# Splitting q and k for fp32r score products: the duplicated load, VectorE and GpSimd, or one load, ScalarE, VectorE and DMAs between partitions

## The chip, the core and the metric

The kernel runs on one core of a Trainium2 chip. The metric is the device time of one execution in microseconds; lower is better. A run's time is the median of several executions.

## What is computed

Attention over 8 batches of 8 heads, 576 positions and 64 channels a head, with a learned bias on relative positions, then a mixture of 8 experts of which each token uses one:

```python
scores = q @ k.T / sqrt(64) + bias        # bias: a small MLP of log1p|i-j| / log1p(max(i,1))
attn = softmax(scores)
x = (attn @ v) laid out as 4608 tokens x 512
e = argmax(x @ w_gate)
out = softmax_prob(e) * (relu(x @ w1[e]) @ w2[e])
```

Everything is float32. The score products run in the faster fp32r form, which keeps fewer bits; so q and k are split into a rounded part and a remainder, and the products of the parts are added up.

## The kernel before

**The stages.** The first 109 us make the bias for all heads (`bias_group`, 36 groups of 16 rows) and, between them, the first pairs of heads. Then 28 pairs pass one after another in a pipeline (`attend_units`), the last two pairs interleaved, up to about 745 us; then come the experts (`Experts`).

**One pair.** A pair is two heads of one batch, five tiles of q rows (four of 128, one of 64). For each tile and head: four score products of 128 x 288 into PSUM (`product`, line 163); VectorE adds the bias and takes the row minimum (line 168); ScalarE takes the exponential and the row sum (line 171); TensorE transposes the result (208, 203), ScalarE and VectorE copy it to SBUF (214, 204, 212, 210); TensorE multiplies it with v (219, 222). The steps of neighbouring tiles overlap: the transposes of one tile stand behind the score products of the next. The `s` tiles in PSUM and the `tps` tiles have two buffers each.

**q and k.** In HBM both lie transposed, with the two heads side by side (1216 columns), and the 64 channels twice, in partitions 0 to 63 and 64 to 127. `load_qk` (lines 125 to 143) loads each with one DMA of 608 KB. VectorE casts k to fp32r (line 138); GpSimd subtracts that from k in the upper 64 partitions (139), so that `k1` holds the rounded part above the remainder. VectorE casts q (141), GpSimd subtracts it in all partitions (142): `q1` is the rounded part twice, `q2` the remainder twice. A product with `q1` and one with `q2`, each over 128 partitions, add up to all four products of parts. `q1`, `q2`, `k1` and `v` have two buffers (pool `kq`), the raw tiles two (pool `raw`).

**What sets the order.** `ahead` asks for `load_qk` of the next pair at the second q tile of a pair, and for `load_v` at the fourth. The framework's scheduler then orders the instructions of each engine, and inserts the waits; each engine works through its list in order. All these loads stand on SP's queue. The framework has eight completion semaphores for the DMAs, so a DMA can wait for the one eight before it on that queue.

Of the kernel before, what the change touches and what calls it, by code (L numbers as in the profile page):

```python
# [10 lines left out]
F32 = mybir.dt.float32  # L11
F32R = mybir.dt.float32r
I32 = mybir.dt.int32
AF = mybir.ActivationFunctionType
ALU = mybir.AluOpType
# [5 lines left out]
P = 128  # L21
B, H, S, D = 8, 8, 576, 64
SH = S // 2
NPAIR = H // 2
# [4 lines left out]
QT = len(QN)  # L29
KC = DM // P  # L30
FC = FF // P
KW = 2 * S + 64
NG = S // 16
XW = DM + 4

# [42 lines left out]
def attention(tc, ctx, q, kt, vm, ltab, bcst, gate, gt, cm, cmat, ival, tail0, pcst, bias, xs, plan, moe):  # L78
    nc = tc.nc
    ident, before, ones = gt[:, 0, :P], cm[:, 0], cm[:, 1]  # L80
    kq = ctx.enter_context(tc.tile_pool(name="kq", bufs=2))
    raw = ctx.enter_context(tc.tile_pool(name="raw", bufs=2))
    tp = ctx.enter_context(tc.tile_pool(name="tp", bufs=2))
    ap = ctx.enter_context(tc.tile_pool(name="ap", bufs=2))
    const = ctx.enter_context(tc.tile_pool(name="aconst", bufs=1))
# [28 lines left out]
    loaded = {}  # L114

    def load_pair(b, pr):
        load_qk(b, pr)
        load_v(b, pr)
# [6 lines left out]
    def load_qk(b, pr):  # L125
        u = b * NPAIR + pr

        def twice(src):

            t = raw.tile([P, KW], F32, name="qk")  # L130
            nc.sync.dma_start(out=t, in_=src[b, pr])
            return t

        q1 = kq.tile([P, KW], F32R, name="q1")
        q2 = kq.tile([P, KW], F32R, name="q2")
        k1 = kq.tile([P, KW], F32R, name="k1")
        t = twice(kt)
        nc.vector.tensor_copy(out=k1, in_=t)  # L138
        nc.gpsimd.tensor_tensor(out=k1[64:128], in0=t[64:128], in1=k1[64:128].bitcast(F32), op=ALU.subtract)  # L139
        t = twice(q)  # L140
        nc.vector.tensor_copy(out=q1, in_=t)  # L141
        nc.gpsimd.tensor_tensor(out=q2, in0=t, in1=q1.bitcast(F32), op=ALU.subtract)  # L142
        loaded[u] = (q1, q2, k1)

    xsb = {}

    def scores(b, pr, qt):

        q1, q2, k1, v = loaded[b * NPAIR + pr]
        n = QN[qt]  # L150
        q0 = qt * P
        if (b, qt) not in xsb:
            xsb[b, qt] = xp[b % 2].tile([P, XW], F32, name="xrow")
        a = ap.tile([P, 2 * S], F32, name="a")
# [3 lines left out]
        def product(hf, hh, second, first, last):  # L158
            if n < P:
                i, k0 = (S - n, S)[hh], (0, KW - S)[hh]  # L160
            else:
                i, k0 = (0, KW - 512)[hh] + q0, S * hh
            return nc.tensor.matmul(s[:, hf, :SH], (q1, q2)[second][:, i:i + P], k1[:, k0 + hf * SH:k0 + hf * SH + SH], start=first, stop=last)  # L163

        def weights(m, hh, bt):

# [6 lines left out]
        if n < P:  # L173
            s = ps_s.tile([P, 2, 512], F32, name="s")
# [8 lines left out]
        for hh in range(2):  # L183
            s = ps_s.tile([P, 2, 512], F32, name="s")
# [301 lines left out]
    with ExitStack() as es:  # L486
        atp = [es.enter_context(tc.tile_pool(name="atp", bufs=2)), es.enter_context(tc.tile_pool(name="osb", bufs=2)), P]
        bp = es.enter_context(tc.tile_pool(name="bp", bufs=1))
        hp = es.enter_context(tc.tile_pool(name="hp", bufs=8))
        op = es.enter_context(tc.tile_pool(name="op", bufs=3))  # L490
        lt = bp.tile([P, 1152], F32, name="lt")
        bc = bp.tile([P, 4 * NG + 2 + 4 * H], F32, name="bc")
# [101 lines left out]
    last = attend_units(units, ahead, after)  # L594
    advance(100)
    plan_experts()
    s = []
# [238 lines left out]
def layout(inputs):  # L836

    q, k, v = inputs["q"], inputs["k"], inputs["v"]

    q, k = (a.reshape(B, NPAIR, 2, S, D).transpose(0, 1, 4, 2, 3).reshape(B, NPAIR, D, 2 * S) for a in (q, k))  # L840

    q = q.reshape(B, NPAIR, D, 2, S).copy()
    q[..., S - 64:] = q[..., S - 64:].reshape(B, NPAIR, D, 2, 8, 8).swapaxes(-1, -2).reshape(B, NPAIR, D, 2, 64)
    q = np.concatenate([q[..., 0, :], np.zeros_like(q[..., 0, :64]), q[..., 1, 512:], q[..., 1, :512]], axis=-1)
    k = np.concatenate([k, k[..., S:S + KW - 2 * S]], axis=-1)

    q, k = (np.concatenate([a, a], axis=2) for a in (q, k))
    vv = v.reshape(B, NPAIR, 2, S, D)
    vm = np.zeros((B, NPAIR, P, 5, P), v.dtype)
    for hh in range(2):  # L850
        h = slice(64 * hh, 64 * hh + 64)
# [8 lines left out]
    t = np.arange(1152)  # L860
    ltab = np.log1p(np.abs(t[None, :] - (S - 1) - 8 * ii[:, None]).astype(np.float32)).astype(np.float32)
    i = np.array([row_base(G, j) for G in range(NG) for j in range(4)])[None, :] + 8 * ii[:, None]
# [42 lines left out]
```

## Time and profile before

| | us |
|---|---|
| median of 3 runs | 1237.55 (1236.25 to 1239.64) |
| the profiled execution | 1246.06 |
| its span, first to last instruction | 1244.2 |
| TensorE matmuls busy | 1111.9 (89%) |
| TensorE weight loads busy | 893.6 (72%) |
| VectorE busy | 776.5 (62%) |
| ScalarE busy | 524.4 (42%) |
| GpSimd busy | 347.3 (28%) |
| 124.57 MB moved by DMA | 100 GB/s over the span |

The shares are means over stages that differ; VectorE for instance is at 80 to 90% up to about 745 us and at about 30% behind it. A busy TensorE isn't TensorE at its peak, because matmuls overlap in it. Names: PE is TensorE's matmuls, PEld its weight loads, DVE is VectorE, ACT is ScalarE, POOL is GpSimd, SP is SyncE, whose queue starts the DMAs.

### The profile page before, as it was taken

The page shows a single profiled execution, that of the slowest core. Times are in us where ns is not written, and L with a number is a line of the kernel's source. Part 1 is how long each engine was busy: PE and PEld are TensorE (multiplying, and loading weights), DVE is VectorE, ACT ScalarE, POOL GpSimd, SP SyncE. Part 2 cuts the span into 40 slices and gives each one's busy share as a digit, 9 for nine tenths or more (in the row PEclk, how much of TensorE's full clock was granted, in tenths as well). Part 3 has the DMA queues.
Part 4 walks back from the last instruction along what each step waited for, and adds up shares of the span by engine and source line. Part 5 has one row for each costly group of instructions (what it writes and reads, how often), then busy time and mean ns, then how long its engine had stood idle before and what let it go on. Part 6 is the DMA issues. An engine that isn't in the chain of part 4 may idle for free. (4 is left out here: it accounts for less than half of the span.)

```text
span 1244.2 us, 20226 instructions
## 1 busy us (share of the span) xinstructions
PE 1111.9 (89%) x7332; PEld 893.6 (72%) x7332; DVE 776.5 (62%) x2025; ACT 524.4 (42%) x1251; POOL 347.3 (28%) x288
## 2 busy tenths in 40 slices
PE   7898888989898888889898899799989899989894
PEld 3457666767666666667676688688978799978782
DVE  8987888898888888887878786232323322324141
ACT  5885655646455555555464463111211211213130
POOL 3003325143333242242333332330005040032320
PEclk8998999999999999999999999899999999999897
DMA  8544213223232232141232241720151610252400
GB/s 237 149 121 122 88 65 110 82 73 119 72 107 78 79 101 92 62 130 62 91 101 87 67 160 65 280 81 26 34 186 44 210 67 23 71 189 68 162 18 26
DMA packets 39362, 124.57 MB, mean 100 GB/s; under 512 B 5154, under 2 KB 5666, under 8 KB 39074
## 3 DMA queue, kind: packets, MB, share of 16 engines
q1 hardware_dynamic: 32962, 102.86, 26.2%
q0 software_dynamic: 5920, 18.95, 4.1%
q8 instruction: 72, 1.18, 0.4%
q14 instruction: 120, 0.98, 0.3%
q10 hardware_dynamic: 288, 0.59, 0.1%
HBM read 92.82 MB, written 23.97 MB: 94 GB/s over the span
## 5 line engine op out<-in xcount | busy, mean ns | idle before, releaser
L171 ACT ACTIVATE a<-t,mn 128x576 f32<-128x576 f32 x288 | 223.8, 777 | 168.1 <-DVE mn L168 126.7
L163 PE MATMUL s<-k,q 128*128 128x288 f32 x1280 | 242.1, 327 | 41.6 <-DVE mn L168 27.4
L163 PEld LDWEIGHTS s<-k,q 128*128 128x128 f32 x1280 | 188.0, 194 | 102.3 <-DVE mn L168 48.0
L168 DVE CUSTOM_DVE_ANT_0 t<-s,bias 128x576 f32<-128x576 f32 x288 | 211.4, 749 | 53.3 <-PE s L163 40.2
L691 PE MATMUL psh<-bias,bias 128*128 128x384 f32 (+2 forms) x1248 | 210.0, 326 | 23.8 <-issue 23.2
L691 PEld LDWEIGHTS psh<-bias,bias 128*128 128x128 f32 x1248 | 202.3, 198 | 29.5 <-issue 25.1
L208 PE MATMUL tps<-gt,a 128*128 128x128 f32 x1152 | 165.6, 283 | 37.5 <-DVE r L237 24.6
L142 POOL TENSOR_TENSOR q<-qk,q 128x1216 fp32r<-128x1216 f32 x32 | 90.0, 2814 | 322.0 <-DVE q L141 181.9
L208 PEld LDWEIGHTS tps<-gt,a 128*128 128x128 f32 x1152 | 136.5, 146 | 52.2 <-issue 45.0
L681 ACT ACTIVATE bias<-psh 128x384 fp32r<-128x384 f32 (+2 forms) x104 | 46.7, 451 | 266.1 <-PE psh L691 263.4
L222 PE MATMUL o<-at,v 128*64 128x320 f32 (+3 forms) x1216 | 156.0, 383 | 0.0
L682 DVE SCALAR_TENSOR_TENSOR bias<-psh,bias 128x384 fp32r<-128x384 f32 (+2 forms) x104 | 51.9, 505 | 112.0 <-ACT bias L681 111.7
L730 POOL DMA_INDIRECT out<-y,ids x38 | 37.3, 981 | 302.0 <-DVE y L729 281.3
L222 PEld LDWEIGHTS o<-at,v 128*64 128x64 f32 x1216 | 71.5, 138 | 52.1 <-issue 27.7
L139 POOL TENSOR_TENSOR k<-qk,k 64x1216 fp32r<-64x1216 f32 x32 | 88.9, 2777 | 43.9 <-DVE k L138 26.6
L212 DVE COPY at<-tps 128x512 f32<-128x512 f32 x128 | 87.7, 685 | 16.9 <-PE o L222 10.8
L725 PE MATMUL psy<-w2h,bias 128*128 128x512 f32 (+1 forms) x224 | 88.8, 398 | 0.0
L726 PE MATMUL psy<-w2l,bias 128*128 128x512 f32 (+1 forms) x224 | 88.2, 396 | 0.0
L138 DVE CAST k<-qk 128x1216 fp32r<-128x1216 f32 x32 | 88.0, 2749 | 0.0
L727 PE MATMUL psy<-w2h,bias 128*128 128x512 f32 (+1 forms) x224 | 87.2, 397 | 0.0
L729 DVE TENSOR_SCALAR y<-psy,g 128x512 f32<-128x512 f32 (+1 forms) x38 | 28.4, 748 | 91.3 <-PE psy L727 91.3
L214 ACT COPY at<-tps 128x512 f32<-128x512 f32 x128 | 73.3, 573 | 27.9 <-PE tps L208 26.3
(164 smaller groups left out, 1460.9 us busy)
## 6 DMA issues: line engine op xcount, KB each, us to landing
qk<-in_kt SPq DMA_DIRECT2D x32, 608.0 KB, 3.8
qk<-in_q SPq DMA_DIRECT2D x32, 608.0 KB, 3.8
bias<-in_wl SPq DMA_DIRECT2D x28, 512.0 KB, 3.7
v<-in_vm SPq DMA_DIRECT2D x32, 320.0 KB, 2.9
wr<-in_wl SPq DMA_DIRECT2D x20, 512.0 KB, 8.2
xg<-xs SPq DMA_DIRECT2D x12, 774.0 KB, 8.3
bias<-ob SPq DMA_DIRECT2D x32, 288.0 KB, 3.2
xs<-in_none SPq DMA_DIRECT2D x6, 774.0 KB, 4.8
```

What stands on the lines that cost most here:

```text
L138: nc.vector.tensor_copy(out=k1, in_=t)
L139: nc.gpsimd.tensor_tensor(out=k1[64:128], in0=t[64:128], in1=k1[64:128].bitcast(F32), op=ALU.subtract)
L142: nc.gpsimd.tensor_tensor(out=q2, in0=t, in1=q1.bitcast(F32), op=ALU.subtract)
L163: return nc.tensor.matmul(s[:, hf, :SH], (q1, q2)[second][:, i:i + P], k1[:, k0 + hf * SH:k0 + hf * SH + SH], start=first, stop=last)
L168: nc.vector.tensor_tensor_reduce(out=t[:m], in0=s[:m, :, :SH], in1=bt.rearrange("p (a c) -> p a c", a=2), op0=ALU.add, op1=ALU.min, scale= ...
L171: nc.scalar.activation(out=a[:m, hh * S:(hh + 1) * S], in_=t[:m].rearrange("p a c -> p (a c)"), func=AF.Exp, bias=mn[:m, hh:hh + 1], scale ...
L208: mm = nc.tensor.transpose(tps[:, c], a[:, k0:k0 + P], ident)
L212: nc.vector.tensor_copy(out=at[:, 4:8, c0:c0 + n], in_=tps)
L222: mm = nc.tensor.matmul(o[64 * hh:64 * hh + 64, :N], v[:, c, 64 * hh:64 * hh + 64], at[:, 4 * hh + c, :N], start=False, stop=c == 3, skip_ ...
L691: nc.tensor.matmul(ps[:, :N], w[c][:, k0:k0 + P], x[kc][:, :N], start=i + kc == 0, stop=i == 2 and kc == KC - 1)
L725: nc.tensor.matmul(ps[:n], a, wh, start=f == 0, stop=False)
L726: nc.tensor.matmul(ps[:n], a, wo, start=False, stop=False)
```

## The change

q and k are loaded once, in their own layout: the two heads of a pair one above the other in 128 partitions, 704 columns for q and 640 for k. ScalarE makes the rounded part `hi`, VectorE the remainder in place of the raw tile, for both heads at a time. DMAs then move 64 partitions each to where the products want them: `qs` holds, for each head, the rounded q above the remainder; `k1` holds the rounded k twice, `k2` the remainder twice. A product with `k1` and one with `k2` add up to the same four products of parts. That is twelve DMAs a pair, 4 of 64 x 704 and 8 of 64 x 640 elements. The pool `raw` has one buffer for each of `qn`, `kn` and `hi`, and `hi` serves q and then k. The pool `hp` of the bias stage has seven buffers instead of eight. GpSimd has no part in it any more.

```diff
-KW = 2 * S + 64
+QW, KW = S + 2 * 64, S + 64
...
-    raw = ctx.enter_context(tc.tile_pool(name="raw", bufs=2))
+    raw = ctx.enter_context(tc.tile_pool(name="raw", bufs=1))
...
-        q1 = kq.tile([P, KW], F32R, name="q1")
-        q2 = kq.tile([P, KW], F32R, name="q2")
-        k1 = kq.tile([P, KW], F32R, name="k1")
-        t = twice(kt)
-        nc.vector.tensor_copy(out=k1, in_=t)
-        nc.gpsimd.tensor_tensor(out=k1[64:128], in0=t[64:128], in1=k1[64:128].bitcast(F32), op=ALU.subtract)
-        t = twice(q)
-        nc.vector.tensor_copy(out=q1, in_=t)
-        nc.gpsimd.tensor_tensor(out=q2, in0=t, in1=q1.bitcast(F32), op=ALU.subtract)
-        loaded[u] = (q1, q2, k1)
+        qn = raw.tile([P, QW], F32, name="qn")
+        kn = raw.tile([P, KW], F32, name="kn")
+        nc.sync.dma_start(out=qn, in_=q[b, pr])
+        nc.sync.dma_start(out=kn, in_=kt[b, pr])
+        qs = kq.tile([P, 2, QW], F32R, name="qs")
+        k1 = kq.tile([P, 2, KW], F32R, name="k1")
+        k2 = kq.tile([P, 2, KW], F32R, name="k2")
+        for src, places in ((qn, ([(qs, 0)], [(qs, 1)])), (kn, ([(k1, 0), (k1, 1)], [(k2, 0), (k2, 1)]))):
+            hi = raw.tile([P, QW], F32R, name="hi")[:, :src.shape[-1]]
+            nc.scalar.copy(out=hi, in_=src)
+            nc.vector.tensor_tensor(out=src.bitcast(F32R), in0=src, in1=hi.bitcast(F32), op=ALU.subtract)
+            for part, tiles in zip((hi.bitcast(F32), src), places):
+                for t, half in tiles:
+                    for h in range(2):
+                        nc.sync.dma_start(out=t[64 * half:64 * half + 64, h].bitcast(F32), in_=part[64 * h:64 * h + 64])
+        loaded[u] = (qs, k1, k2)
...
-                i, k0 = (0, KW - 512)[hh] + q0, S * hh
-            return nc.tensor.matmul(s[:, hf, :SH], (q1, q2)[second][:, i:i + P], k1[:, k0 + hf * SH:k0 + hf * SH + SH], start=first, stop=last)
+                i, k0 = q0, 0
+            return nc.tensor.matmul(s[:, hf, :SH], qs[:, hh, i:i + P], (k1, k2)[second][:, hh, k0 + hf * SH:k0 + hf * SH + SH], start=first, stop=last)
...
-        hp = es.enter_context(tc.tile_pool(name="hp", bufs=8))
+        hp = es.enter_context(tc.tile_pool(name="hp", bufs=7))
```

The scheduler places the new instructions. VectorE, before, where one pair ends and the next begins (`r` is of the fourth and fifth q tile, `t_2589` the weights of the fifth, `t_2616` of the next pair's first):

```order
L241 TENSOR_SCALAR r_2522<-r_2522 128x2
L242 RECIPROCAL r_2522<-r_2522 128x2
L141 CAST q1_2642<-qk_2649 128x1216
L168 ISA t_2589,mn_2575<-s_2577,bias4_71 128x576
L168 ISA mn_2575 128x1
L138 CAST k1_2644<-qk_2645 128x1216
L212 COPY at_2542<-tps_2598 128x4x128
L237 TENSOR_SCALAR r_2576<-r_2576 128x1
L168 ISA t_2616,mn_2609<-s_2611,bias0_67 128x576
```

Both casts stood here, on either side of the fifth tile's weights. VectorE now, in the same place of a pair (lines have moved by two; line 170 is the weights):

```order
L170 ISA t_2728,mn_2721<-s_2723,bias0_67 128x576
L170 ISA mn_2721 128x1
L170 ISA t_2739,mn_2721<-s_2734,bias0_67 128x576
L170 ISA mn_2721 128x1
L140 TENSOR_TENSOR kn_2755<-kn_2755,hi_2768 128x640
L212 COPY at_2654<-tps_2742 128x8x64
L243 TENSOR_SCALAR r_2722<-r_2722 128x2
```

The subtraction of k stands behind the next pair's first tile; that of q stands one and a half tiles earlier in the pair, ahead of the fourth tile's weights. ScalarE now, at the end of a pair (`a_2686` is the fifth tile, `a_2720` the next pair's first; before, the copy followed the fifth tile's exponential at once):

```order
L173 ACTIVATE a_2686,r_2688<-t_2701,mn_2687 128x576
L139 CAST hi_2768<-kn_2755 128x640
L206 COPY at_2654<-tps_2731 128x128
L173 ACTIVATE a_2720,r_2722<-t_2728,mn_2721 128x576
L173 ACTIVATE a_2720,r_2722<-t_2739,mn_2721 128x576
L309 COPY osb_2752<-o_2684 128x256
```

A cast of k has come in ahead of the next pair's exponentials; the cast of q comes in behind the third tile's. SP now, for one pair, with its waits (`PE` on `v` is the buffer of v, on `qs` that of the pair before last; `DMAHW` are completions of earlier DMAs):

```order
L133 DMA kn<-in_kt 128x640 [waits DMAHW4_49,DMAHW2_49,DMAHW7_49,DMAHW1_49,DMAHW0_49]
L122 DMA v<-in_vm 128x640 [waits DMAHW5_49,PE_49]
L144 DMA qs<-hi 64x704 [waits DMAHW6_49,PE_49,Activation_49]
L144 DMA qs<-hi 64x704
L144 DMA qs<-qn 64x704 [waits DVE_49]
L144 DMA qs<-qn 64x704
L144 DMA k_2759<-hi 64x640 [waits Activation_49]
L144 DMA k_2759<-hi 64x640 [waits DMAHW3_49]
L144 DMA k_2759<-hi 64x640 [waits DMAHW4_49]
L144 DMA k_2759<-hi 64x640 [waits DMAHW5_49]
L144 DMA k_2760<-kn 64x640 [waits DMAHW6_49,DVE_49]
```

Three more of the last kind follow, then the load of the next pair's q. Before, SP held three rows a pair: the loads of k, of q and of v.

## Rows read from the trace of the kernel before

**Rows 1.** Busy time by stage: us, PE, PEld, DVE, ACT, POOL, granted clock, DMA share, GB/s.
```profile
108.90:697.30 588.40, 522.49 (x3616) 401.25 (x3617) 489.71 (x1394) 326.25 (x851) 196.88 (x162) 0.97 0.28 89
```
**Rows 2.** The same for four pairs, cut 0.5 us ahead of VectorE's cast of k.
```profile
294.28:313.75 19.47, 17.77 (x129) 13.68 (x127) 16.12 (x47) 11.59 (x31) 5.56 (x2) 1.00 0.28 82
313.75:334.96 21.21, 19.42 (x130) 14.45 (x128) 16.75 (x48) 11.92 (x31) 5.55 (x2) 0.92 0.24 76
334.96:357.47 22.51, 19.20 (x129) 15.27 (x129) 19.37 (x57) 11.53 (x32) 7.28 (x13) 0.92 0.23 71
357.47:379.33 21.86, 18.92 (x132) 13.98 (x131) 18.41 (x52) 11.71 (x31) 10.40 (x8) 1.00 0.38 127
```
**Rows 3.** The same for 7 us around that cast, and for what follows once.
```profile
294.28:301.28 7.00, 5.30 (x40) 3.76 (x39) 6.65 (x13) 3.48 (x10) 5.56 (x2) 1.00 0.29 89
...
334.96:341.96 7.00, 3.94 (x30) 2.58 (x29) 7.00 (x7) 1.39 (x4) 5.54 (x2) 1.00 0.29 89
...
301.28:313.75 12.47, 12.47 (x91) 9.92 (x90) 9.47 (x35) 8.11 (x23) 0.00 (x0) 1.00 0.27 78
```
**Rows 4.** Waits of PE, 108.9 to 697.3 us: us in total, times, longest.
```profile
PE tps L208 <- DVE r L237: 24.6, 14, 1.9
PE s L163 <- DVE mn L168: 21.8, 16, 3.6
PE s L163 <- DVE r L237: 9.9, 3, 3.3
```
**Rows 5.** Single lines, whole span: duration in ns, shortest/median/longest.
```profile
L138 DVE CAST k<-qk x32: 772/2996/3087, 9.0 to 698.4; 128x1216 fp32r<-128x1216 f32 x32
...
L141 DVE CAST q<-qk x32: 769/794/795, 13.7 to 697.0; 128x1216 fp32r<-128x1216 f32 x32
...
L381 DVE TENSOR_TENSOR oh<-lgsum,mx x8: 202/2311/2314, 170.5 to 758.7; 128x40 f32<-128x40 f32 x8
```
**Rows 6.** Timeline, 440 to 465 us: start, us, engine, line.
```profile
441.35 0.75 DVE L168 CUSTOM_DVE_ANT_0 t<-s,bias 128x576 f32<-128x576 f32 x1
...
441.57 2.78 POOL L142 TENSOR_TENSOR q<-qk,q 128x1216 fp32r<-128x1216 f32 x1
...
442.02 2.98 DVE L138 CAST k<-qk 128x1216 fp32r<-128x1216 f32 x1
...
442.20 0.78 ACT L171 ACTIVATE a<-t,mn 128x576 f32<-128x576 f32 x1 [0.32 <-DVE mn L168]
...
452.57 0.78 ACT L171 ACTIVATE a<-t,mn 128x576 f32<-128x576 f32 x1
...
453.25 0.19 ACT L171 ACTIVATION_READ_ACCUMULATOR a<-t,mn 128x1 f32 x1
...
454.93 1.10 PE L208 MATMUL tps<-gt,a 128*128 128x128 f32 x8
```
**Rows 7.** Groups of instructions by line and form: count, us busy, mean ns, idle before.
```profile
L653 DVE TENSOR_TENSOR bias<-bias,bias 128x1024 fp32r<-128x1024 f32 x20 | 24.5, 1226 | 8.1 <-ACT bias L652 8.1
...
L652 ACT CAST bias<-bias 128x1024 fp32r<-128x1024 f32 x20 | 20.8, 1042 | 0.0
```
**Rows 8.** DMA issues: KB each and median us to landing; two lines by themselves.
```profile
v<-in_vm SPq DMA_DIRECT2D x32, 320.0 KB, 2.9
...
bias<-ob SPq DMA_DIRECT2D x32, 288.0 KB, 3.2
...
bias<-ob SPq DMA_DIRECT2D x4, 144.0 KB, 4.3
...
L131 SPq DMA_DIRECT2D qk<-in_kt x32: 327/328/432, 2.2 to 678.1; - x32
...
DMA to landing us min/median/max: 3.1/3.2/6.6
```
**Rows 9.** The start: stretch of 40 us (columns as above), and a wait of PE.
```profile
0.00:40.00 40.00, 30.73 (x250) 12.61 (x254) 35.73 (x55) 23.39 (x32) 13.09 (x20) 0.87 0.80 228
...
PE s L532 <- DVE h L527: 7.1, 4, 2.3
```

More of the change, by code (lines that the diff above doesn't have):

```diff
@@ L126, in load_qk @@
         u = b * NPAIR + pr
[L128 to L132, printed above, removed]
-        q1 = kq.tile([P, KW], F32R, name="q1")
-        q2 = kq.tile([P, KW], F32R, name="q2")
-        k1 = kq.tile([P, KW], F32R, name="k1")
-        t = twice(kt)
-        nc.vector.tensor_copy(out=k1, in_=t)
-        nc.gpsimd.tensor_tensor(out=k1[64:128], in0=t[64:128], in1=k1[64:128].bitcast(F32), op=ALU.subtract)
-        t = twice(q)
-        nc.vector.tensor_copy(out=q1, in_=t)
-        nc.gpsimd.tensor_tensor(out=q2, in0=t, in1=q1.bitcast(F32), op=ALU.subtract)
-        loaded[u] = (q1, q2, k1)
+        qn = raw.tile([P, QW], F32, name="qn")
[14 more added lines that the diff above has]
+        loaded[u] = (qs, k1, k2)
     xsb = {}
     def scores(b, pr, qt):
-        q1, q2, k1, v = loaded[b * NPAIR + pr]
+        qs, k1, k2, v = loaded[b * NPAIR + pr]
         n = QN[qt]
@@ L838, in layout @@
     q, k, v = inputs["q"], inputs["k"], inputs["v"]
[L840 to L847, printed above, removed]
+    q, k = (a.reshape(B, NPAIR, 2, S, D).swapaxes(-1, -2) for a in (q, k))
+    q = q.copy()
+    q[..., S - 64:] = q[..., S - 64:].reshape(B, NPAIR, 2, D, 8, 8).swapaxes(-1, -2).reshape(B, NPAIR, 2, D, 64)
+    q = np.concatenate([q, np.zeros_like(q[..., :64]), q[..., S - 64:]], axis=-1).reshape(B, NPAIR, 2 * D, QW)
+    k = np.concatenate([k, k[..., :64]], axis=-1).reshape(B, NPAIR, 2 * D, KW)
     vv = v.reshape(B, NPAIR, 2, S, D)
```

## The prediction

> **What bounds the kernel now.** First the busy time by stage. Between 108.90 and 697.30 us, where 28 pairs of heads pass, TensorE is busy 522.49 of 588.40 us, VectorE 489.71 and ScalarE 326.25 [rows 1]. TensorE is the fullest, but 588.40 - 522.49 = 65.9 us of it lie idle, 2.35 us a pair, and the question is who takes them. Second, single pairs: they come in groups of four, of 19.47, 21.21, 22.51 and 21.86 us, with 17.77 to 19.42 us of matmuls in each [rows 2]; 28 such pairs make 588.4 us, 21.0 on average. Third, the place inside a pair: in the 7 us from half a microsecond before VectorE's cast of k, TensorE works 5.30 or 3.94 us and VectorE 6.65 or 7.00, while the 12.47 us behind the first of these are full of matmuls to the last digit, with VectorE at 9.47 [rows 3]. So the pipeline can run without a gap, and loses its time in one place. Fourth, the waits of TensorE: in the stretch the longest are all for VectorE, 24.6 + 21.8 + 9.9 = 56.3 us [rows 4]; the smaller ones name a VectorE copy. Fifth, the cause: the cast of k takes 2996 ns in the median and 772 at its shortest, the cast of q with the same shape 794 [rows 5]. In the timeline that cast starts at 442.02 and ends at 445.00, while GpSimd's subtraction runs from 441.57 to 444.35 [rows 6]: VectorE stands behind GpSimd. The routing step shows the same on a tiny operation, 202 ns at its shortest and 2311 in the median [rows 5].
>
> **What the change removes.** 32 casts of k, 32 of q on VectorE, and 64 subtractions on GpSimd. With the subtractions goes what holds VectorE up. In the stretch TensorE's 65.9 us of idle time are all put down to VectorE; VectorE falls from 17.5 us a pair (489.71 / 28) by 3.0 + 0.79, gains the subtractions below (1.6), and loses a blocked routing operation in two of four pairs (2 us each): about 14.3 of 18. **Term a: -65.9 us.**
>
> **TensorE's clock.** In the first and fourth pair of a group the granted clock is 1.00, in the second and third 0.92, so part of these is spent at 1.2 GHz instead of 2.4 [rows 2]. The second and third have 19.42 and 19.20 us of matmuls for nearly the same count as the first's 17.77: 1.65 + 1.43 = 3.08 us a group, 21.6 in seven groups. The third stands for 7.00 - 3.94 = 3.1 us of the seven around the cast, but the first stands for 1.7 too and keeps its clock [rows 3], so the idle time is not the whole story. Bounds 0 and -21.6; I take -18, since the gaps mostly go. **Term b: -18.**
>
> **What is added on VectorE and ScalarE.** A subtraction of 704 and one of 640 elements: by 1226 ns for 1024 on VectorE [rows 7], 0.84 + 0.77 us. A cast of each on ScalarE: by 1042 ns for 1024 [rows 7], 0.72 + 0.65. ScalarE goes from 11.7 us a pair to 13.0, VectorE to the 14.3 above; both stay under TensorE's 18. They lie beside the matmuls and cost nothing by their length; if TensorE ever gets faster than some 14 us a pair, that cover is gone.
>
> **The new wait.** The rounded copy, hi, has one buffer, used for q and then for k. So ScalarE's cast of k waits until both DMAs that carry q's rounded part away have landed; these wait for the last score product of the pair before last, whose qs buffer they fill. In the new order that cast stands behind the exponential of the last q tile, ahead of a copy and the two exponentials of the next pair's first tile: all of these are held. Call the end of that last product T. VectorE's weights start 0.1 later (an estimate of the hand-over), the exponential 0.85 after them (441.35 to 442.20), and takes 0.78 + 0.19: it ends at T + 1.9 [rows 6]. SP issues from T + 0.1, 0.33 us each [rows 8], so the second DMA starts at T + 0.43 and lands L later. ScalarE stands for 0.43 + L - 1.9, then casts for 0.65: the exponentials come L - 0.8 us later than without the change. How much of that is hidden: in a full stretch the second exponential of a tile ends at 453.44 and its transposes begin half way through the eight at 454.93, so at 455.48 [rows 6]: 2.0 us of slack. TensorE then stands for L - 2.8 a pair. For L no row has just this transfer (160 to 176 KB, SBUF to SBUF). Nearest: 288 KB from SBUF to SBUF, 3.2; 320 KB from HBM, 2.9; the first of three issued in a row, 144 KB, 4.3 [rows 8]. I take 3.3, the 3.2 and a little for the second standing behind the first: 0.5 us a pair, 14 in all. Bounds 3 (at 2.9) and 42 (at 4.3, 1.5 us a pair); the longest of the 288 KB ones, 6.6 [rows 8], is a rival's. **Term c: +14.**
>
> The Trainium skill ("DMA: Bandwidth & Descriptors", Anatomy of one DMA) fits a DMA as 2.0 us plus the bytes over 436 GB/s, for the other kind of queue; for 180 KB that is an estimate of 2.4 us, TensorE would not wait at all, and the sum would be 14 us lower. The same formula gives 2.7 us for the 288 KB that the rows show at 3.2, so here the row decides.
>
> **The queues.** Per pair SP issues 15 DMAs where it issued 3: 12 x 0.33 = 4 us more of SP, which is idle otherwise. Ahead of the q parts stands the load of v, which waits for products that end before T; behind the k parts stand the next q and k, with one raw buffer each. The parts of k leave after ScalarE's cast (T + 4.5) and VectorE's subtraction (about T + 5.3), and have landed by some T + 10; they are needed one pair after T, at about T + 18. The next q is loaded from about T + 7 and cast around T + 12. Nothing here is late, with 8 us to spare. The bytes: parts 4 x 64 x 704 x 4 + 8 x 64 x 640 x 4 = 2.03 MB, loads 0.69, v 0.33: 3.05 MB a pair, where it was 1.57. At 228 GB/s for a share of 0.80 [rows 9], 285 at full share, that is 10.7 us of 18.
>
> **The end of attention and the start.** The last pair's cast, at 698 us, loses its 3 us too: **term d, -2** (0 to -3). At the start VectorE makes the bias, and TensorE waits 7.1 us for it there [rows 9]; against that, two pairs bring 2 x (2.72 - 1.25) = 2.94 MB more, 10.3 us at 285 GB/s, into 40 us that have 8 us of the DMA engines free. The bias groups lose one of eight buffers, which makes every third element-wise step wait for products two groups back; it falls inside the same bounds. **Term e: +2** (-7 to +10). The matmuls are the same in number and shape, and the experts' stage is not touched: 0.
>
> **Sum:** -65.9 - 18 + 14 - 2 + 2 = -69.9. The profiled execution took 1246.06 us (1244.2 in the span, 1.9 around it), and would take 1176.2; it lies 8.5 above the median of the runs shown, 1237.55, so the median would be **1167.7**. That is 18.5 us a pair: 18.0 of matmuls and 0.5 of waiting.
>
> **Rivals.** *ScalarE is held longer, and the clock stays.* With L = 4.3 and term b at 0: -65.9 + 42 - 2 + 2 = -24, 1214. For it: four DMAs leave together, and the row of three leaving together shows 4.3. Against: in the stretch the DMA engines are busy 0.28, and those DMAs take longer to issue. Chance 0.2.
>
> *ScalarE is held so long that it replaces VectorE as the one that stalls.* The point is L - 2.8 > 2.35, so L over 5.15 us. With the 6.6 seen once, term b at 0 and d and e cancelling: 3.8 x 28 = 106, and -65.9 + 106 = +40: 1278. For it: the engine blocks in order, and everything behind it is on the path. Against: 6.6 belongs to the start, with the DMA engines near full. Chance 0.08.
>
> *The DMA engines become the bound.* By the rows they need 10.7 us a pair. The Trainium skill ("DMA: Bandwidth & Descriptors", Bandwidth) lists 138 GB/s for transfers of 64 KB and 341 for 1 MB. The mechanism is this kernel's: twelve small transfers instead of two of 608 KB. If they ran at under 145 GB/s, 3.05 MB would need over 21 us and a pair could not be shorter than now; at 138 it is 22.1 us, 1.1 x 28 = 30 more, 1268. The 134 GB/s that the bias writes moved took only about half of the engines' time, so I give it 0.02.
>
> *Better:* L under 2.8, the whole clock and a quicker start, down to 1140. Chance 0.06. *No change,* ends that cancel: 0.02. That GpSimd still has a part is ruled out by the new order, which has no subtraction there.
>
> **How the numbers follow.** The forecast, 1148 to 1190, has 0.62. The range from 1146 to 1220 holds it and the first rival; outside are the two slower cases and the edges, under 0.2. A measurement tells 0.3% from no change, here 3.7 us. Faster by more: 0.62 + 0.2 + 0.06 = 0.88; slower 0.08 and part of the DMA case: 0.09; the same: 0.03.
>
> **What would show it.** Right: between the first and the last pair TensorE over 96% busy; pairs of about 18.5 us; the routing operation at 0.2 us; no wait of TensorE for VectorE over 1 us. Term c: ScalarE idle before its cast of k, put down to a DMA, about 1.8 us each, and TensorE waiting 0.5 behind it. Term b: a granted clock near 1.00 in every pair. Wrong: TensorE waiting for the parts of q or k themselves; a cast of k held for over 3.7 us; a subtraction on VectorE that takes 2 us with no GpSimd beside it; a first pair of scores later than 46 us.

## The result and the profile after

The changed kernel takes **1198.88 us** (median of 4 runs, 1193.65 to 1203.47), the kernel before 1238.60 beside it (4 runs, 1236.25 to 1241.41): a ratio of **0.9677, 95% interval 0.9621 to 0.9734**. That is 39.7 us less, where 69.9 were forecast; 1198.88 lies inside the range, 31 us from the predicted 1167.7, and outside the forecast's own band of 1148 to 1190. The profiled execution took 1203.04 us, 1201.3 of it in the span.

First the busy time by stage of the kernel after, with the columns of [rows 1]: the stretch that answers to [rows 1], the 23 pairs in the middle of it, and two single pairs as in [rows 2].

```profile
108.90:700.00 591.10, 565.56 (x4048) 432.53 (x4047) 449.99 (x1529) 386.29 (x994) 55.85 (x115) 0.99 0.66 178
210.83:641.37 430.54, 420.32 (x2948) 317.59 (x2948) 336.66 (x1146) 290.24 (x742) 38.06 (x85) 1.00 0.67 181
324.00:342.01 18.01, 17.92 (x130) 13.67 (x129) 15.16 (x53) 12.59 (x33) 0.00 (x0) 1.00 0.66 172
398.40:416.43 18.03, 17.60 (x127) 13.38 (x124) 14.66 (x53) 12.60 (x33) 0.00 (x0) 1.00 0.67 171
```

The steady part is about what was forecast: 430.54 us for 23 pairs are 18.72 a pair, TensorE is busy 97.6% of them at a granted clock of 1.00, and 10.2 us are idle, 0.44 a pair. Over the whole of the first row it is 95.7% (565.56 / 591.10), just under the 96% that the prediction named as a sign. Next its waits in that stretch (us in total, times, longest), with ScalarE's before its cast:

```profile
PE tps L210 <- ACT at L206: 5.7, 7, 2.4
PE s L165 <- DVE mn L170: 1.7, 2, 1.1
PE tps L210 <- DVE at L212: 0.7, 2, 0.3
ACT hi L139 <- DMA qs<-hi: 43.3, 24, 2.8
```

In the kernel before, TensorE's waits for VectorE in this same stretch, shorter than that of [rows 4], were:

```profile
PE tps L208 <- DVE r L237: 19.1, 11, 1.8
PE s L163 <- DVE mn L168: 13.6, 12, 3.3
PE s L163 <- DVE r L237: 9.9, 3, 3.3
```

Of these 42.6 us for VectorE's minima (`mn`) and the row sums (`r`) 1.7 are left, the longest 1.1 (the prediction's sign allowed 1); most of what remains is ScalarE's copy of the transposed weights, late behind the cast of k in 7 places. ScalarE stands before that cast for 43.3 / 24 = 1.8 us, put down to the DMA of q's rounded part. The new operations' durations (ns, shortest/median/longest), and the routing operation of [rows 5]:

```profile
L139 ACT CAST hi<-qn x32: 767/782/785, 8.4 to 651.6; 128x704 fp32r<-128x704 f32 x32
L140 DVE TENSOR_TENSOR qn<-qn,hi x32: 884/893/894, 10.0 to 652.4; 128x704 fp32r<-128x704 f32 x32
L383 DVE TENSOR_TENSOR oh<-lgsum,mx x8: 188/195/202, 190.5 to 715.1; 128x40 f32<-128x40 f32 x8
```

Neither the subtractions nor the routing operation stand behind GpSimd any more (the latter takes 195 ns, where the median was 2311). So why 31 us short? First the start; the third and fourth pair, which fell short by as much, come further down. The same windows as in [rows 9], then 10 us at a time:

```profile
0.00:40.00 40.00, 26.74 (x211) 10.28 (x214) 23.62 (x48) 22.73 (x32) 1.22 (x16) 0.78 0.92 223
20.00:30.00 10.00, 4.73 (x32) 1.47 (x32) 3.68 (x7) 5.25 (x7) 0.00 (x0) 0.67 0.90 208
30.00:40.00 10.00, 7.19 (x51) 2.06 (x54) 4.75 (x9) 4.88 (x8) 0.00 (x0) 0.50 1.02 212
40.00:50.00 10.00, 5.29 (x49) 2.44 (x48) 6.21 (x13) 5.25 (x7) 0.00 (x0) 0.84 1.06 227
```

From 20 to 50 us the DMA engines are full (a share of 0.90 to 1.06), TensorE works 17.2 us of 30, and its granted clock is 0.50 to 0.84. The first exponential of the scores, in ScalarE's timeline, comes at 54.58 us:

```profile
51.62 0.74 ACT L536 ACTIVATE ob<-s,cb 128x576 f32<-128x576 f32 x1 [2.22 <-DMA bias<-ob]
...
54.58 0.78 ACT L173 ACTIVATE a<-t,mn 128x576 f32<-128x576 f32 x1 [0.92 <-DVE mn L170]
```

The 288 exponentials, nine to a pair of heads, make a ruler by which kernels can be laid side by side. The first two pairs are worked on alternately with the groups of the bias, so the nineteenth exponential opens the third pair. Starts in us, from the timelines of ScalarE:

| exponential | before | after | difference |
|---|---|---|---|
| 1st | 43.4 | 54.6 | +11.2 |
| 19th (third pair) | 114.8 | 129.0 | +14.1 |
| 37th (fifth pair) | 151.4 | 174.2 | +22.9 |
| 271st (31st pair) | 705.2 | 660.6 | -44.6 |
| end of the span | 1244.2 | 1201.3 | -42.9 |

From the 37th to the 271st exponential, 26 pairs, the change gains 67.5 us. It had lost 14.1 before the third pair and 8.7 more in the third and fourth, and loses 1.7 at the end.

### The profile page after: what moved, and what is told of

Read it like the earlier page. It is cut to its first block, busy times and chain, and to the rows that moved or that the text cites. A ratio compares the mean times of both kernels' runs of the same rounds, so it can differ in the third digit from the quotient of the medians.

```text
span 1201.3 us, 21037 instructions
## 1 busy us (share of the span) xinstructions
PE 1111.0 (92%) x7332; PEld 883.0 (74%) x7332; DVE 680.7 (57%) x2025; ACT 558.3 (46%) x1315; POOL 168.6 (14%) x224
## 5 line engine op out<-in xcount | busy, mean ns | idle before, releaser
L165 PE MATMUL s<-k,qs 128*128 128x288 f32 x1280 | 238.9, 322 | 16.0 <-ACT ob L536 7.8
L165 PEld LDWEIGHTS s<-k,qs 128*128 128x128 f32 x1280 | 184.8, 191 | 75.6 <-issue 32.3
L210 PEld LDWEIGHTS tps<-gt,a 128*128 128x128 f32 x1152 | 131.4, 142 | 35.8 <-ACT at L206 13.1
L394 POOL TENSOR_TENSOR cs<-cs,oh 128x8 f32<-128x8 f32 x40 | 8.0, 201 | 512.8 <-DVE oh L389 510.4
L534 PE MATMUL s<-h,bc 128*32 128x288 f32 x576 | 59.2, 469 | 12.2 <-ACT ob L536 10.3
L668 ACT CAST bias<-tps 128x384 fp32r<-128x384 f32 (+2 forms) x60 | 24.9, 461 | 87.8 <-PE tps L666 78.4
```

Source lines behind the costliest of these rows:

```text
L165: return nc.tensor.matmul(s[:, hf, :SH], qs[:, hh, i:i + P], (k1, k2)[second][:, hh, k0 + hf * SH:k0 + hf * SH + SH], start=first, stop=last)
L210: mm = nc.tensor.transpose(tps[:, c], a[:, k0:k0 + P], ident)
L534: nc.tensor.matmul(ps[32 * j:32 * j + 32, hf, :SH], w2bd, hs[j][:, hf * SH:(hf + 1) * SH], start=True, stop=True)
```

## Experiments on the start

Four theories were set up for the lost start. **A**: the bytes of the parts fill the DMA engines. **B**: on SP's queue the writes of the bias stand behind the parts. **C**: seven tiles h instead of eight. **D**: ScalarE is held before its casts, in order. The table has all kernels (times of single runs are from one profiled run; each group stands beside its own runs of the kernel before).

| kernel | 1st | 19th | 37th | 271st | time | before beside it |
|---|---|---|---|---|---|---|
| before, seven tiles h | 45.5 | 116.2 | 155.8 | 709.5 | 1250.4 | 1236.4 |
| before, more bytes | 54.8 | 117.5 | 157.2 | 713.8 | 1255.7 | 1248.0 |
| before, both | 57.0 | 126.0 | 164.2 | 718.8 | 1259.2 | 1242.3 |
| before, no subtractions | 44.8 | 111.2 | 143.8 | 606.0 | 1161.4 | 1248.0 |
| change, first parts on GpSimd's queue | 47.7 | 127.0 | 161.9 | 642.7 | 1188.9 | 1236.4 |
| change, two buffers hi | 56.7 | 130.7 | 167.4 | 681.5 | 1226.9 | 1236.4 |
| change, eight h, two ob | 58.0 | 135.9 | 180.6 | 662.1 | 1203.4 | 1242.3 |
| change, first three pairs from copies | 43.8 | 114.5 | 155.8 | 641.1 | 1180.0 | 1236.4 |
| the same, later parts on GpSimd's queue | 43.7 | 114.5 | 153.0 | 637.6 | 1184.9 | 1248.0 |
| all pairs from copies | 45.0 | 115.0 | 151.8 | 627.1 | 1167.6 | 1248.0 |
| the same, timed | 43.4 | 115.3 | 157.8 | 631.0 | 1167.8 | 1242.3 |

**Seven tiles alone.**

```diff
-        hp = es.enter_context(tc.tile_pool(name="hp", bufs=8))
+        hp = es.enter_context(tc.tile_pool(name="hp", bufs=7))
```

> The kernel before with seven tiles h for the bias groups instead of eight, and nothing else. It asks whether the lost start comes from the eighth tile (theory C). In the trace of before the first exponential of the scores starts at 43.4 us and the one that opens the third pair (the nineteenth) at 114.8 us; with the change they are at 54.6 and 129.0. C expects about 50 to 55 and 125 to 129 here, and a time some 10 us above that of before; theory A (the bytes of the parts fill the DMA engines until 50 us), B (the writes of the bias stand behind the parts on SP's queue) and D (ScalarE, held before its casts, is late with everything behind them) all expect 43 to 45 and 114 to 117, and the time of before within 3 us.

Measured: 45.5 and 116.2 us, +2.1 and +1.4. By themselves the seven tiles are not the lost start. The single time, 1250.4, compares with the 1246.06 of before's profiled execution: +4.4, about the +4.3 at the 271st exponential. It is 14.0 above the median beside it, but one execution says little: by the traces the 26 pairs take as long as in the kernel before (553.7 against 553.9 us).

**The first parts on another queue.**

```diff
-                        nc.sync.dma_start(out=t[64 * half:...
+                        (nc.gpsimd if u < 3 else nc.sync).dma_start(out=t[64 * half:...
```

> The changed kernel with the twelve DMAs of the parts of each of the first three pairs on GpSimd's queue instead of SP's, so that the writes of the bias and the loads behind them are issued without standing behind parts; the bytes are the same. B expects the first exponential back at 45 to 48 us and the nineteenth at 117 to 121; A expects both as with the change, 52 to 57 and 127 to 132, since the same bytes cross the same DMA engines; D expects them as with the change or a little earlier (a part that is issued sooner lands sooner), 50 to 55. From the fourth pair on all expect the change's 18.7 us a pair.

Measured: the first exponential at 47.7, as B said, but the nineteenth at 127.0, as A said. The queue's order decides which work comes first, not when all of it is done: the exponentials start 7 us sooner and the third pair 2 us sooner. B falls as the cause of the 14 us, though not of the late first exponential.

**A buffer of its own for k's rounded part.**

```diff
-            hi = raw.tile([P, QW], F32R, name="hi")[:, :src.shape[-1]]
+            hi = raw.tile([P, src.shape[-1]], F32R, name="hiq" if src is qn else "hik")
...
-        hp = es.enter_context(tc.tile_pool(name="hp", bufs=7))
+        hp = es.enter_context(tc.tile_pool(name="hp", bufs=6))
```

> The changed kernel with a buffer hi of its own for k (name hik) beside that of q (hiq), so that the cast of k waits for no part of q; the room comes from the bias groups' tiles h, six instead of seven. The forecast's term c says that the wait of some 1.8 us before the cast of k goes, and with it most of the 0.5 us a pair in which TensorE waits: a pair of 18.2 to 18.6 us instead of 18.72 over the 23 pairs of the steady stretch, 3 to 10 us in all. D expects the start to come back too: first exponential at 46 to 51 us, nineteenth at 118 to 124, and the third and fourth pair, 45.2 us together with the change, at 38 to 40. A and B expect the start as with the change (52 to 57, 127 to 132).

Measured: 56.7 and 130.7 us at the start, where D expected 46 to 51 and 118 to 124. That speaks against D but doesn't settle it, since the six tiles h could hide a gain there; the run with more bytes, below, settles it for the first exponential. And a time of 1226.9, slower by far, against every expectation. The wait that was to go did go, and the pairs became longer: 681.5 - 167.4 = 514.1 us for 26 pairs, 19.8 each. The same waits as above, of this kernel, over the same stretch:

```profile
PE tps L210 <- ACT at L206: 27.7, 21, 2.2
ACT hiq L139 <- DMA qn<-in_q: 20.1, 15, 3.0
ACT hik L139 <- DMA kn<-in_kt: 16.0, 18, 1.7
```

TensorE waits 27.7 us for ScalarE's copies instead of 5.7. The timeline shows where the cast now stands:

```profile
418.23 0.78 ACT L173 ACTIVATE a<-t,mn 128x576 f32<-128x576 f32 x1
...
419.78 0.73 ACT L139 CAST hik<-kn 128x640 fp32r<-128x640 f32 x1 [0.68 <-DMA kn<-in_kt]
...
420.88 0.79 ACT L173 ACTIVATE a<-t,mn 128x576 f32<-128x576 f32 x1
```

Nothing holds it until q's parts have landed, so in the new order it comes two microseconds after q's, between the two exponentials of one tile, and waits there for the load of k. With the change, ScalarE's casts of q and k are half a pair apart. The six tiles h differ too, but they act only up to the third pair, not on the 26 pairs. No run changes the order alone, so that it costs the 1.1 us a pair is read from these rows, not shown by itself. One thing did get faster: the third and fourth pair took 36.8 us (D expected 38 to 40), against 45.2 with the change.

**The first three pairs without parts.** Two more inputs hold the first batch's q and k with each head on both halves of the partitions; each head is loaded, cast straight into place, and subtracted.

```diff
+        if u < 3:
+            for h in range(2):
+                kn = raw.tile([P, KW], F32, name="kn")
+                nc.sync.dma_start(out=kn, in_=kd[b, pr, :, h])
+                qn = raw.tile([P, QW], F32, name="qn")
+                nc.sync.dma_start(out=qn, in_=qd[b, pr, :, h])
+                nc.scalar.copy(out=k1[:, h], in_=kn)
+                nc.vector.tensor_tensor(out=k2[:, h], in0=kn, in1=k1[:, h].bitcast(F32), op=ALU.subtract)
+                nc.scalar.copy(out=qs[:, h], in_=qn)
+                nc.vector.tensor_tensor(out=qs[64:128, h], in0=qn[64:128], in1=qs[64:128, h].bitcast(F32), op=ALU.subtract)
```

> The changed kernel, but the first three pairs are loaded head by head from copies in HBM that hold each head on both halves of the partitions, and split straight into qs, k1 and k2: no part is moved by DMA for them. That is 1.38 MB a pair through the DMA engines instead of 2.72 MB, and eight DMAs' fewer issues on SP, for two casts and two subtractions more of each kind. A expects most of the start back: two pairs less 2.7 MB are 12 us at the 222 GB/s of the first 54.6 us, so the first exponential at 43 to 47 us, the nineteenth at 114 to 120, and a time 8 to 16 us below the change's 1198.9. B expects the same here, and is told apart by the kernel with the parts on GpSimd's queue. C expects the start to stay lost (54 and 129). D, with more work on ScalarE but none of its waits for parts, expects something between, 48 to 52.

Measured: the whole start is back, 43.8 and 114.5 us, and the time is 1179.97 (1176.24 to 1182.83; ratio 0.9532, 0.9486 to 0.9578). It still has seven tiles h, so C alone falls once more; what went with the parts, bytes or issues, is the cause.

**More bytes, in the kernel before.**

```diff
+        for h in range(2 if u < 2 else 0):
+            for c in range(4):
+                nc.sync.dma_start(out=bias[4 - u].rearrange("p h s -> p (h s)")[64 * h:64 * h + 64, 704 * c:704 * c + 704], in_=q1[64 * h:64 * h + 64, :704].bitcast(F32))
```

> The kernel before with eight more DMAs of 176 KB behind the casts of each of the first two pairs, from q1 into tiles of the bias that are written much later: 1.44 MB more a pair, about what the change adds there (2.72 MB against 1.25), and nothing else is changed. If bytes and issues through DMA engines that are already busy are what the start lost (theories A and B), the first exponential moves from 43.4 us to 50 to 57 and the nineteenth from 114.8 to 124 to 130, and the time rises by 9 to 15 us above the 1236 of before. If ScalarE's casts are (D), or the seven tiles (C, which the run above put at 2 us for the first exponential and 1.4 for the nineteenth), both stay within 3 us.

Measured: the first exponential at 54.8, the change's 54.6 almost to the digit, with no cast on ScalarE and eight tiles: neither C nor D is needed for it. Bytes (A) and the place on the queue (B) aren't told apart here, since these DMAs stand on SP's queue too; with the first parts on GpSimd's queue the first exponential came at 47.7, which speaks for B there, and the nineteenth at 127.0, which speaks for A. But in this kernel the nineteenth is at 117.5, not 124 to 130. The kernel before, so delayed, catches up.

**Both together.** The same edit with `bufs=7` for the tiles h.

> The kernel before with both at once: the eight more DMAs of 176 KB for each of the first two pairs, and seven tiles h instead of eight. Alone the bytes moved the first exponential by 11.4 us (to 54.8) and the nineteenth by 2.7 (to 117.5): TensorE made up for the late start between 60 and 100 us, with 445 matmuls on record there against 408 in the kernel before. Alone the seven tiles moved them by 2.1 and 1.4, and every kernel with seven has 391 to 398 matmuls on record from 60 to 100 us. The theory that both together are the lost start (the bytes lose it, and with seven tiles TensorE can't make up for it, since VectorE waits for a free tile h) expects the first exponential at 53 to 58 us and the nineteenth at 126 to 131, under 405 matmuls from 60 to 100 us, and a time 10 to 16 us above before's. If the two only add up, the nineteenth comes at 117 to 121.

Measured: 57.0 and 126.0 us, +13.6 and +11.2, where the two alone had given +2.7 and +1.4 at the nineteenth. From 60 to 100 us, once the first exponentials run, by windows: first the bytes alone, then both, then the change, each with VectorE's wait for a free tile h in that stretch.

```profile
60.00:100.00 40.00, 38.81 (x443) 22.74 (x436) 36.26 (x89) 35.24 (x65) 0.00 (x0) 1.00 0.50 130
...
DVE h L530 <- PE s L535: 1.3, 4, 0.3
```

```profile
60.00:100.00 40.00, 39.25 (x393) 21.18 (x392) 32.46 (x81) 31.89 (x58) 0.00 (x0) 1.00 0.46 117
...
DVE h L530 <- PE s L535: 7.2, 8, 1.4
```

```profile
60.00:100.00 40.00, 39.25 (x387) 21.38 (x387) 32.51 (x80) 32.00 (x59) 0.00 (x0) 1.00 0.46 118
...
DVE h L529 <- PE s L534: 7.2, 8, 1.4
```

With eight tiles TensorE gets through 443 matmuls on record in these 40 us, with seven through 393, and the change's row is the second's twin: 387 matmuls, the same 39.25 us, the same 7.2 us of VectorE waiting. In the same 40 us the kernel before, which is not late, has 407, and all six kernels with seven tiles, late or not, have 386 to 394. So the start is lost to the added DMAs and **kept** lost with seven tiles: 11.2 of the change's 14.1 us by these two. The other 2.9 us no run accounts for. How a matmul comes to take more of TensorE's time with seven tiles (39.25 / 393 = 100 ns against 88) isn't settled; the order of the bias groups' products differs, and some records are missing.

**Eight tiles again, in the changed kernel.** The room comes from the output tiles of the groups.

```diff
-        hp = es.enter_context(tc.tile_pool(name="hp", bufs=7))
-        op = es.enter_context(tc.tile_pool(name="op", bufs=3))
+        hp = es.enter_context(tc.tile_pool(name="hp", bufs=8))
+        op = es.enter_context(tc.tile_pool(name="op", bufs=2))
```

> The changed kernel with eight tiles h again; the room for the eighth comes from the output tiles ob of the bias groups, two instead of three. The theory of both together expects the first exponential late as with the change (52 to 57 us), but the nineteenth back at 117 to 122 instead of 129.0, with 420 or more matmuls on record from 60 to 100 us instead of 395, and a time 6 to 12 us below the change's. That seven tiles have no part in it expects 127 to 131 and the change's time. Against it stands that with two tiles ob a bias group may wait for the write of the one before it: then the first exponential comes later still, 57 to 62 us, and the gain is eaten.

Measured: 58.0 and 135.9 us, and 1203.39 us (1198.12 to 1207.70; ratio 0.9704, 0.9641 to 0.9767), which can't be told from the change. The caution in the last sentence came true, and worse than it said: from 0 to 130 us ScalarE waits 18.3 us in 14 waits for the writes of the bias, against 11.0 in 8 with the change. From 60 to 100 us 400 matmuls are on record, under the 420 expected. This run doesn't test the eighth tile by itself in the changed kernel; there is no room for that, so it stays with the kernel before.

## Experiments on the steady part, and the best version

**GpSimd's subtractions left out of the kernel before.** The remainders of q and k are left out of the products. This gives the forecast's terms a and b by themselves.

```diff
-        nc.gpsimd.tensor_tensor(out=k1[64:128], in0=t[64:128], ...
-        nc.gpsimd.tensor_tensor(out=q2, in0=t, in1=q1.bitcast(F32), op=ALU.subtract)
-        loaded[u] = (q1, q2, k1)
+        loaded[u] = (q1, q1, k1)
```

> The kernel before without GpSimd's two subtractions of each pair; VectorE's casts stay, and q1 stands where q2 stood, so the remainders of q and k are left out of the products. It asks for the forecast's terms a and b alone: GpSimd's part goes, and no cast, transfer or issue comes in its place. The forecast's reason (VectorE stands behind GpSimd, and TensorE behind VectorE) expects the pairs from the fifth on, 21.3 us each in the trace of before (the exponentials number 37 to 271 in 553.8 us over 26 pairs), at 18.0 to 18.6 us, a granted clock of 0.99 or 1.00 in that stretch, and a time 70 to 84 us below the 1236 of before. The rival, that VectorE's own work is what TensorE waits for and GpSimd only happens to run beside it, expects 20 us a pair or more and less than 40 us off the time. The start changes by less than 3 us by the first and by theory A.

Measured: 606.0 - 143.8 = 462.2 us for the 26 pairs, 17.8 each, against 553.8: **-91.6 us**. The stretch of 23 pairs' length above, in this kernel:

```profile
210.83:641.37 430.54, 428.58 (x3153) 334.30 (x3154) 348.43 (x1211) 275.96 (x730) 48.96 (x99) 1.00 0.33 111
```

TensorE is idle 2.0 us of 430.54, at the full clock: what held it was VectorE behind GpSimd, and the clock came back (0.97 in this stretch before) as the gaps went. The 26 pairs are a steady measure: the three other kernels made from the kernel before take 553.7 to 556.5 us for them. VectorE's own work, 348.43 us, holds nobody up for long: no wait of TensorE for VectorE is on record there. The time, 1161.4, says less than the pairs do: behind the last exponential this kernel needs 514.8 us to the end of the span against 499.7, presumably because products without remainders send other tokens to the experts.

**All pairs from copies.** No part is moved by DMA anywhere; the casts of ScalarE and the subtractions of VectorE are twice as many, and the eighth tile h has room again.

```diff
+        qd = raw.tile([P, 2, QW], F32, name="qd")
+        nc.sync.dma_start(out=qd, in_=q[b, pr])
...
+        for h in range(2):
+            nc.scalar.copy(out=qs[:, h], in_=qd[:, h])
+            nc.vector.tensor_tensor(out=qs[64:128, h], in0=qd[64:128, h], in1=qs[64:128, h].bitcast(F32), op=ALU.subtract)
+        kd = raw.tile([P, 2, QW], F32, name="qd")[:, :, :KW]
+        nc.sync.dma_start(out=kd, in_=kt[b, pr])
+        for h in range(2):
+            nc.scalar.copy(out=k1[:, h], in_=kd[:, h])
+            nc.vector.tensor_tensor(out=k2[:, h], in0=kd[:, h], in1=k1[:, h].bitcast(F32), op=ALU.subtract)
```

> All pairs loaded from copies in HBM that hold each head on both halves of the partitions, cast by ScalarE straight into qs and k1 and subtracted by VectorE: no part is moved by DMA anywhere, and each pair has two casts (0.78 and 0.73 us) and two subtractions (0.89 and 0.83) more than with the change; the bias groups have their eight tiles again. Theory A expects the start of the kernel before: first exponential at 43 to 48 us, nineteenth at 114 to 119. In the steady stretch two readings part: if TensorE is the bound with slack beside it (VectorE at 14.6 us of 18.72 would come to 16.4, ScalarE at 12.6 to 14.1), a pair stays at 18.5 to 18.9 us and the time is 1175 to 1186; if the exponentials and evictions stand behind the casts in ScalarE's and VectorE's order, as they did in the kernel with two buffers hi (a pair of 19.8 us), a pair takes 19.3 to 20.5 us and the time is above 1195.

Measured: 45.0 and 115.0 us at the start, as A said; 627.1 - 151.8 = 475.3 us for the 26 pairs, **18.3** each, less than the lower end of either reading; 1167.6 us. Its stretch:

```profile
210.83:641.37 430.54, 425.62 (x3020) 323.70 (x3017) 379.90 (x1225) 326.00 (x802) 53.38 (x97) 1.00 0.35 113
```

VectorE is busy 88% and ScalarE 76%, more than with the change, and yet TensorE is idle only 4.9 us: the length of their work is covered. This fits the reading that in the kernel with two buffers hi the place of a cast cost the time, not the work. The bytes are down from 181 to 113 GB/s.

**The same, timed.**

> The kernel whose pairs all come from the copies in HBM, without parts, timed. One run gave 1167.6 us beside 1248.0 for the kernel before on that chip, a ratio of 0.936; the change's own ratio is 0.968. All theories expect 0.93 to 0.95 here, and a version that beats both kernels.

Measured: **1167.76 us** (6 runs, 1164.77 to 1170.58) beside 1242.27 (11 runs): a ratio of 0.9412, 0.9368 to 0.9457. It beats both kernels, the change by some 2.7% (0.9412 / 0.9677).

**Later parts on GpSimd's queue.** To the kernel whose first three pairs come from copies, with `nc.gpsimd` for the parts of all others.

> The kernel with the first three pairs loaded from the copies in HBM (1180.0 us), and the parts of all later pairs on GpSimd's queue, so that no load stands behind them on SP's. The third and fourth pair took 41.3 us there, against 34.9 in the kernel whose first parts were on GpSimd's queue and 36.6 in the kernel before. Theory B, confined to these two pairs, expects 35 to 38 us for them and a time of 1172 to 1177. If what is lost there is the landing of the loads (bytes), it expects 40 to 43 us and 1178 to 1182. Against it stands that GpSimd's own issues may take longer than SP's 0.6 us and delay the parts; a pair of the steady stretch would then rise above 18.8 us and the time above 1183.

Measured: 38.5 us for the third and fourth pair, between the two expectations, and 18.6 us a pair behind them; 1184.89 us (1180.21 to 1187.70) with a ratio of 0.9494, 0.9445 to 0.9542, whose interval holds the 0.9532 of the kernel it was made from. Inconclusive: if the queue of the later parts matters, it is by less than these intervals.

**The third and fourth pair.** The change loses 8.7 us there (45.2 against 36.6). In its timeline ScalarE stands 5.2 us before a cast of q, put down to the parts of k: `hi` has one buffer for both, so q's cast must wait until k's rounded part has been carried away. Without the hold that cast would start 4.6 us after the one of k; in the steady stretch 9.3 us lie between two such casts (324.00 to 333.28), and there no hold is on record. Behind it TensorE stands 3.1 us for a copy of ScalarE's, and its granted clock falls:

```profile
160.93 0.78 ACT L139 CAST hi<-qn 128x704 fp32r<-128x704 f32 x1 [5.23 <-DMA k<-hi]
...
163.00 2.37 PE L210 MATMUL tps<-gt,a 128*128 128x128 f32 x8 [3.08 <-ACT at L216]
...
160.00:170.00 10.00, 6.86 (x28) 5.62 (x29) 4.48 (x17) 5.64 (x14) 0.00 (x0) 0.66 0.31 85
```

The kernel with eight tiles h and two ob, which differs from the change in the bias stage alone, shows the same hold, and 44.7 us for the two pairs:

```profile
167.18 0.78 ACT L139 CAST hi<-qn 128x704 fp32r<-128x704 f32 x1 [5.02 <-DMA k<-kn]
```

Where the hold is gone or short, so is the loss: with a buffer of its own for k's rounded part 36.8 us, with the first parts on GpSimd's queue (a hold of 0.3 us) 35.0. With the first three pairs from copies it is 4.8 us, and the two pairs take 41.3. So this hold is the likeliest cause. It is not shown alone, because these two pairs vary from one execution to the next: the kernel with all pairs from copies, which has no `hi`, took 36.8 us in one trace and 42.5 in the other, with the same program. One row of the waits, from 115 us to the fifth pair, first trace and second:

```profile
ACT k L141 <- DMA qd<-in_kt: 1.5, 2, 1.2
```

```profile
ACT k L141 <- DMA qd<-in_kt: 5.3, 2, 3.7
```

There a load landed later, and ScalarE, in order, held everything behind its cast. Of the change itself there is only one trace, so how often it loses the 8.7 us stays open.

## Why the prediction was half right

The forecast gave every pair the same gain, 69.9 / 28 = 2.5 us. In the span it fell short by 27.0 us (42.9 gained for 69.9): 12.1 at the start (+14.1 for +2), 13.7 in the third and fourth pair (+8.7 for -5.0) and 3.7 at the end (+1.7 for -2), while the 26 other pairs gained 2.6 more than their 64.9. The remaining 4 us of the 31 come from the step from one profiled execution to the median, taken as 8.5 and 4.2 in the kernel after.

**Terms a and b** (-65.9 and -18): right in cause, a little small. The run without GpSimd's subtractions gives -91.6 us for 26 pairs, 3.5 a pair, where the forecast had 83.9 / 28 = 3.0. The granted clock went from 0.97 to 1.00 as the gaps went, as said.

**Term c** (+14): right in place, too small in all. ScalarE stands 1.8 us before the cast of k, and TensorE idles 0.44 us a pair, both as forecast (1.8 and 0.5), though TensorE's idle time comes in a few longer waits, 7 for ScalarE's copy in 23 pairs, and not in every pair. But against the run without subtractions the change costs 486.4 - 462.2 = 24.2 us in 26 pairs, 0.93 a pair: TensorE's matmuls fill 18.3 us of a pair instead of 17.7, which the forecast had at 18.0 in any case. Waiting is 0.36 of the 0.93; why the matmuls take 0.57 longer at the same granted clock of 1.00 no run shows. The errors of a, b and c cancel: -67.5 measured for 26 pairs, where 26 / 28 of the forecast's -69.9 are -64.9. That is luck in part. The landing was taken at 3.3 us, above the rows for the parts of q in the steady stretch (KB each, median us to landing):

```profile
qs<-hi SPq DMA_DIRECT2D x46, 176.0 KB, 2.6
qs<-qn SPq DMA_DIRECT2D x46, 176.0 KB, 3.1
```

The hold of 1.8 us came out right all the same, since SP's issue, taken at 0.33 us, measured nearly twice that: two parts of q in 1.11 us and four of k in 2.39. The kernel before had a nearer row than the one taken, the writes of the bias from SBUF to SBUF, at 0.53 (last line):

```profile
324.75 2.39 SPq L144 DMA_DIRECT2D k<-hi  x4
...
338.44 1.11 SPq L144 DMA_DIRECT2D qs<-hi  x2
...
342.01 0.73 ACT L139 CAST hi<-kn 128x640 fp32r<-128x640 f32 x1 [1.73 <-DMA qs<-hi]
...
L537 SPq DMA_DIRECT2D bias<-ob x32: 532/532/665, 8.5 to 85.7; - x32
```

From the first issue to the cast this pair takes 3.57 us, where 0.33 + 3.3 = 3.63 were forecast: with 0.55 for the first issue, 3.0 are left for the second DMA to land. One term was too short and the other too long.

The formula of the Trainium skill ("DMA: Bandwidth & Descriptors", Anatomy of one DMA), fitted on the other kind of queue, gave an estimate of 2.4 us for such a transfer; the median of 2.6 is nearer to it than to the 3.3 taken, the 3.0 of this pair lies in the middle. By it TensorE would not have waited at all, and there the trace disagrees.

**The queues.** "Nothing here is late, with 8 us to spare" failed, and this is the step behind the third and fourth pair as far as is known: the prediction priced q's parts holding the cast of k, but not k's parts holding the next cast of q, through the same buffer `hi` (5.2 us in the fourth pair). The twelve issues took 7.2 us of SP (1.11 + 1.23 + 2.39 + 2.46 in one pair) where 4 were forecast, and the load of q, which stands behind them, was late for its cast in most pairs of the steady stretch; what that costs TensorE isn't shown:

```profile
ACT hi L139 <- DMA qn<-in_q: 15.9, 17, 3.1
```

**Term d** (-2) can't be told apart at this size; from the 271st exponential to the end the change loses 1.7 us.

**Term e** (+2, bounds -7 to +10) is the term of the sum that failed: "10.3 us at 285 GB/s, into 40 us that have 8 us of the DMA engines free". Measured: +11.2 at the first exponential and +14.1 at the nineteenth. Three things were wrong in it. The rate: full engines moved 212 to 227 GB/s here, not 285, so the 2.94 MB are 13 to 14 us. The cover: the 8 free microseconds were not where the bytes came; the engines were full from 20 to 50 us. And the seven tiles were put "inside the same bounds": alone they cost 1.4 us and the bytes alone 2.7, together 11.2, since a late start is made up with eight tiles and not with seven. The prediction's own sign for this, a first pair of scores later than 46 us, was there.

**The rivals.** No hold over 3.7 us in the steady part, so neither rival of ScalarE held longer came, though the time, 1198.88, lies between the forecast's band and the first one's 1214: near its number, without its mechanism. The DMA engines as the bound, at 138 GB/s, didn't come either: in the steady stretch they moved 181 at a share of 0.67.

Sum by measured terms, in the span: +14.1 (start) + 8.7 (third and fourth pair) - 67.5 (26 pairs) + 1.7 (end) = -43.0, against 1201.3 - 1244.2 = -42.9. These are stretches of the two traces laid end to end, so they must add up; the sum says where the time went, not why.

## What to carry to other kernels

Price what a change adds to the start by itself, by the rate of the engines where they are full and by where their free time lies, not by its sum; then ask whether the slack that would make it up (a buffer, here) is given away by the same change. A wait on an in-order engine can be what keeps an instruction in a harmless place: before it is removed, look where the instruction would go. Where operands are static, a second layout in HBM may be cheaper than moving parts on the chip, even at twice the element-wise work, as long as the bound engine covers that work.

## What the runs showed of the hardware

What the DMA engines moved for their busy share was not constant: 228 GB/s at a share of 0.80 in the first 40 us before, 212 at 1.02 and 227 at 1.06 in two stretches of the start after. An issue of a part on SP took 0.55 to 0.6 us in the median, and a load of a whole tile in the same trace 0.33 (k), 0.38 (v) or 0.58 (q). A 176 KB part landed in 2.6 to 3.1 us in the median while the engines were 0.67 busy. Within one trace TensorE, with 17.2 us of work in the 30 from 20 to 50 us, had a granted clock of 0.50 in one stretch of 10 us, which is its lower level (1.2 GHz of 2.4), and of 0.67 and 0.84 in the two beside it; from 60 to 120 us, with 57.8 us of work in 60, it had 1.00.
